# Attention and MoE kernel: the turned softmax weights laid out for 512-byte reads, with a second buffer, the last w_in columns kept in SBUF, and a new order of the steps

## The chip, the cores and the metric

The kernel runs on one core of a Trainium2 chip. The metric is the time of one execution on the device in microseconds (us), the median of several runs. One further execution was taken with the hardware profiler; all rows below are from it. The engines are TensorE (PE, with its weight loads PEld), VectorE (DVE), ScalarE (ACT), GpSimd (POOL) and SyncE (SP). Almost all DMAs are issued by SP, from one queue in order.

## The reference

```python
def _attn_ref(x, state):                    # x (8, 8, 512, 64), state (8, 8, 32, 64)
    scale = 1.0 / np.sqrt(D)
    scores = scale * np.matmul(x, state.transpose(0, 1, 3, 2))
    scores = scores - scores.max(-1, keepdims=True)
    a = np.exp(scores)
    a /= a.sum(-1, keepdims=True) + 1e-09
    xread = np.matmul(a, state)
    scores2 = scale * np.matmul(state, x.transpose(0, 1, 3, 2))
    ...
    a2 /= a2.sum(-1, keepdims=True) + 1e-09
    sread = np.matmul(a2, x)
    return np.concatenate([xread, sread], axis=2)

def _moe_ref(x, w_in, w_out):               # x (8 * 544, 512), w_in (512, 2048), w_out (2048, 512)
    h = np.maximum(x @ w_in, 0.0)
    return h * h @ w_out
```

The weights w_in and w_out come as 64-bit floats and are turned into 32-bit ones in the kernel ("decode").

## The kernel before, in words

There are nine blocks of rows: 512 rows of xread for each of the eight batches, and block 8 with the 8 x 32 rows of sread. To have matmuls at the fast rate and near full precision, an operand is split into a rounded part "hi" and the rest "lo", and three products are summed (mm3, L563; split, L539: the hi copy on ACT, the subtraction on POOL or DVE).

xread is never formed: state times w_in is made first ("w2", by batch and by block hb of 256 of the 2048 columns), and hidden (L1065) multiplies it with the softmax weights. w2 comes from three places. Batches 0 and 1: rows direct.hb, right from the decoded w_in tile wf (two_w2, L938). Batches 2 to 5: split_wf (L918) splits w_in, later_w2 (L982) multiplies, results w4ps, stored to DRAM through "o" tiles. Batches 6 and 7: rows w2.hb, from a second reload of w_in, stored as w2l. For the second and third use w_in is read back from DRAM (win_f, written by decode_wi) by load_wf 1 and 2 (L912) into one of two "wf" buffers.

The block hidden.b.fc makes 128 of the 2048 columns for one batch: six matmuls of 512 columns into a PSUM bank (ph, two banks), then on ACT and DVE relu, square, g_hi, and last g_lo, which releases the bank. accumulate.b.fc (L1121) follows with twelve matmuls into acc. Batches 4 to 7 use a form with fewer products (m34, m52, m76, m1).

The sread side: exp_s (L724) gives e, unnormalized. Its matmul with x (read, L811) wants e with positions on the partitions. transposes (L797) does this by way of DRAM: for each of two halves g, DVE transposes e in 32 x 32 blocks into a tile "turned", SP stores it to e_d, then four DMAs read it back as eT. The tile has one buffer:

```python
turned = p2.tile([P, S], F32, tag="turned", name=f"turned{b}_{g}", bufs=1)
nc.vector.transpose(turned, self.e2.pop(g))
nc.sync.dma_start(e_d[b][g], turned)
...
self.eT = p2.tile([P, KC, G * NC, Ns], F32, tag="eT", name=f"eT{b}", bufs=1)
```

Rows of PE (ROWS, L366) join groups of small matmuls that follow each other: scores.b, read.b, direct.hb and w2.hb, each group in one or two PSUM banks of ps_b ("psb") and ps_h ("ph").

The order is written out by hand. PLAN (L25) names the steps one by one; each name runs its step to the next yield, so the instructions of each engine and of SP's queue stand in that order. SECOND (L391) names the instructions that go to the other one of two engines: with decode_wi.p the clamp goes from DVE to POOL, with w_out_lo.fc the subtraction of prep_wo.fc (L1057) from POOL to DVE. Tiles are given out in rings: five "o" buffers for all stored results, two "wraw" buffers for raw w_in and wf_hi. A tile of a ring waits until the last use of its buffer is over; for a stored one that is the landing of its DMA. Nearly every call goes through L447, so profile rows are told apart by their tiles.

Of the kernel before, what the change touches and what calls it, by code (L numbers as in the profile page):

```python
# [25 lines left out]
    ident warm.0 warm.8 warm.19 warm.36 warm.21 start.0 warm.34 warm.29 warm.28 warm.14 load_states.0 load_states.0  # L26
        load_states.0 start.0 load.0.1 neg_ident load.0.1 warm.5 warm.13 prep.0.0 prep.0.0 states.0 states.0
        prep.0.1 prep.0.0 prep.0.1 prep.0.1 prep.0.0 prep.0.1 warm.24 load_raw.0 load_raw.1 start.1 start.1 warm.2
        warm.11 warm.22 load_wo.0 decode_wi.0 decode_wi.0 scores.0 load.1.1 load.1.1 load_raw.2 decode_wi.0
        decode_wi.0 warm.30 warm.32 decode_wi.0 keep_s.0.1 decode_wi.1 decode_wi.1 warm.35 keep_s.0.0 warm.25  # L30
        decode_wi.1 warm.1 decode_wi.1 prep.1.0 load_wo.1 prep.1.0 decode_wi.1 warm.15 transposed_scores.0.1
        transposed_scores.0.0 softmax.0.1 direct_w2.0 warm.33 softmax.0.0 warm.26 warm.23 direct_w2.0 direct_w2.0
        warm.31 softmax.0.1 warm.16 softmax.0.1 softmax.0.0 warm.6 direct_w2.0 direct_w2.0 load_wo.2 warm.37
        direct_w2.0 softmax.0.0 direct_w2.0 second_w2.0 prep_wo.0 softmax.0.1 warm.3 exp_s.0.0 warm.18 softmax.0.0
        prep_wo.0 prep_wo.0 warm.12 warm.20 second_w2.0 second_w2.0 warm.9 warm.4 decode_wi.2 prep.1.1 warm.27
        second_w2.0 second_w2.0 softmax.0.0 prep_wo.0 prep.1.1 load_raw.3 second_w2.0 softmax.0.1 warm.17 warm.7
        decode_wi.2 prep.1.1 prep.1.1 prep.1.0 softmax.0.1 decode_wi.2 decode_wi.2 softmax.0.0 prep.1.0 scores.1
# [24 lines left out]
        direct_w2.3 transposes.0 direct_w2.3 load_wo.12 decode_wi.10 direct_w2.3 direct_w2.3 load_raw.11
        decode_wi.10 decode_wi.10 decode_wi.10 hidden.1.3 hidden.1.3 hidden.1.3 hidden.1.3 hidden.1.3 prep_wo.6
        load_raw.9 decode_wi.8 prep_wo.11 prep_wo.11 prep_wo.11 decode_wi.8 decode_wi.8 second_w2.3 second_w2.3
        second_w2.3 decode_wi.8 states.2 prep_wo.11 hidden.0.7 hidden.0.7 hidden.0.7 prep_wo.11 prep_wo.5
        hidden.0.4 transposes.0 second_w2.3 hidden.0.7 split_states second_w2.3 second_w2.3 hidden.0.4 hidden.0.4
        hidden.0.4 accumulate.1.3 accumulate.1.3 accumulate.1.3 hidden.0.7 hidden.0.7 hidden.0.4 hidden.0.4
        hidden.0.5 accumulate.1.3 accumulate.1.3 accumulate.1.3 decode_wi.11 decode_wi.11 decode_wi.11 decode_wi.11
        decode_wi.8 decode_wi.9 hidden.0.5 hidden.0.5 exp_s.1.0 prep_wo.9 hidden.0.6 hidden.0.5 prep_wo.7
        accumulate.0.4 accumulate.0.4 prep_wo.9 prep_wo.8 decode_wi.9 decode_wi.9 decode_wi.9 decode_wi.11  # L70
        hidden.0.5 hidden.0.5 accumulate.0.5 hidden.0.6 hidden.0.6 hidden.0.6 load_raw.12 load_raw.14 exp_s.1.0
        hidden.0.6 hidden.0.6 decode_wi.9 direct.4+direct.5 prep_wo.8 prep_wo.8 prep_wo.8 load_wo.13 prep_wo.7
        prep_wo.7 prep_wo.8 direct_w2.5 direct_w2.5 direct_w2.5 decode_wi.12 direct_w2.5 exp_s.1.0 direct_w2.4
# [12 lines left out]
        direct_w2.6 decode_wi.14 accumulate.1.7 sread.0 sread.0 sread.0 load_wf.1.0 sread.0 prep_wo.10 hidden.0.9
# [278 lines left out]

ROWS = """  # L366
    scores.0
    scores.1
    direct.4 direct.5
    direct.6 read.0  # L370
    direct.7
    scores.2 read.1
    w2.1 scores.3
    read.2
    w2.0 scores.4
    read.3
    w2.2 scores.5
    w2.5 read.4
    w2.3 scores.6
    w2.6 read.5  # L380
    w2.4 scores.7
    w2.7 read.6
    read.7
"""

# [1223 lines left out]
```

## Time and profile before

| what | value |
|---|---|
| median of 3 runs | 647.99 us (647.28 to 649.07) |
| the profiled execution's own time | 647.67 us |
| its span | 645.9 us |
| PE busy | 631.8 us, 98% |
| DVE, ACT, POOL busy | 474.5, 419.7, 211.4 us |
| DMA | 149343 packets, 105.76 MB; 92960 packets under 512 B |
| HBM read, written | 69.27 MB, 35.65 MB |

The span is what the profiler saw of the engines; the execution's own time has some 1.8 us more around it. Busy time of PE is modelled: a row of a matmul runs into the next one, so that a wait of PE shows shorter than it is. A bracket behind a row of a timeline tells the idle time of the engine before it, and what ended it as far as the profile shows.

### The profile page before, as it was taken

How to read it: one execution, taken by the hardware profiler on the slowest of the kernel's cores; microseconds unless marked ns; L12 is line 12 of the kernel's file. 1: busy time of each engine (PE TensorE's matmuls, PEld its weight loads, DVE VectorE, ACT ScalarE, POOL GpSimd, SP SyncE). 2: the span in 40 equal slices, each digit the busy share in tenths (PEclk: the TensorE clock that was granted, in tenths of full speed). 3: DMA queues.
4: the chain of work that ended last, by engine and by line, in shares of the span. 5: the costliest groups of instructions: out<-in, count | busy, mean ns of one | idle time of the engine just before them, and what ended most of it. 6: DMA issues, size and time to landing. Idle time of an engine off the chain costs nothing.

```text
span 645.9 us, 12786 instructions
## 1 busy us (share of the span) xinstructions
PE 631.8 (98%) x4629; PEld 535.7 (83%) x4629; DVE 474.5 (73%) x968; ACT 419.7 (65%) x882; POOL 211.4 (33%) x206
## 2 busy tenths in 40 slices
PE   9999999999989999899999999999999999999996
PEld 7777767888767777677778888999999999999996
DVE  4999698655855686786677599998767776577556
ACT  4998775654653557455566679887766766667653
POOL 0365343432313142121221140004334275564430
PEclk9999999999999999899999999999999999999999
DMA  8977889988989888999897402120420040003001
GB/s 285 347 258 248 261 248 322 307 226 220 250 223 268 252 216 203 237 269 250 232 257 225 132 2 81 34 83 1 148 82 18 16 131 17 2 26 107 2 2 65
DMA packets 149343, 105.76 MB, mean 164 GB/s; under 512 B 92960, under 2 KB 122144, under 8 KB 149280
## 3 DMA queue, kind: packets, MB, share of 16 engines
q1 hardware_dynamic: 148992, 104.69, 56.5%
q8 instruction: 36, 0.59, 0.4%
q10 hardware_dynamic: 288, 0.26, 0.1%
q14 instruction: 27, 0.22, 0.1%
HBM read 69.27 MB, written 35.65 MB: 162 GB/s over the span
## 4 chain that ended last, share of the span: by engine, by line
PE 75%; DVE 7%; DMA 6%; issue 4%; ACT 3%; SPq 3%; POOL 1%; POOLq 0%; DVEq 0%; ACTq 0%
PE ph L447 25%; PE m L447 23%; PE acc L447 21%; SPq L447 3%; DMA e_d<-turned 2%; PE w2ps L447 2%; DVE wf L447 2%; DMA win_f<-wf 2%; PE w4ps L447 2%; DVE m L447 1%; DMA w_d<-w4o 1%; PE pr L447 1%; DMA wi_raw<-in_moe_w_in_dram 1%; DVE g_lo L447 1%; ACT ph L447 1%
## 5 line engine op out<-in xcount | busy, mean ns | idle before, releaser
L447 PE MATMUL ph<-k_hi,w 128*128 128x512 f32 x512 | 176.8, 394 | 1.3 <-DVE g_lo L447 1.3
L447 PE MATMUL acc<-wo,g_hi 128*128 128x512 f32 x576 | 165.2, 395 | 1.4 <-POOL wo L447 0.9
L447 PEld LDWEIGHTS acc<-wo,g_hi 128*128 128x128 f32 x576 | 107.1, 188 | 28.7 <-issue 3.8
L447 ACT ACTIVATE r<-ph 128x512 f32<-128x512 f32 (+1 forms) x124 | 70.1, 568 | 72.0 <-PE ph L447 68.0
L447 PEld LDWEIGHTS ph<-k_hi,w 128*128 128x128 f32 x512 | 96.5, 188 | 23.4 <-DVE g_lo L447 3.1
L447 PE MATMUL ph<-k_lo,w 128*128 128x512 f32 x256 | 100.5, 392 | 0.0
L447 PE MATMUL acc<-wo,g_lo 128*128 128x512 f32 x288 | 97.7, 393 | 1.9 <-DVE g_lo L447 1.9
L447 PEld LDWEIGHTS acc<-wo,g_lo 128*128 128x128 f32 x288 | 54.1, 189 | 14.3 <-DVE g_lo L447 2.3
L447 DVE TENSOR_TENSOR g_lo<-ph,g_hi 128x512 fp32r<-128x512 f32 (+1 forms) x79 | 49.5, 631 | 22.1 <-ACT g_hi L447 19.5
L447 PEld LDWEIGHTS ph<-k_lo,w 128*128 128x128 f32 x256 | 48.3, 189 | 7.5
L447 POOL TENSOR_TENSOR sp<-sp,m 128x512 f32<-128x512 f32 x22 | 23.3, 1061 | 94.8 <-DVE m L447 81.7
L447 POOL TENSOR_TENSOR w<-w_f,w 128x512 fp32r<-128x512 f32 x19 | 25.2, 1333 | 53.6 <-ACT w L447 35.6
L447 ACT CAST w<-w_f 128x512 fp32r<-128x512 f32 x56 | 34.3, 615 | 7.6 <-PE ph L447 6.0
L447 ACT ACTIVATE g_hi<-r 128x512 fp32r<-128x512 f32 (+1 forms) x60 | 33.9, 570 | 3.9 <-PE acc L447 2.7
L447 ACT ACTIVATE g<-r 128x512 f32<-128x512 f32 x54 | 33.8, 630 | 1.2 <-DVE s4.1.0_5062 L447 0.5
L447 POOL TENSOR_TENSOR wf<-wf,wf_hi 128x512 fp32r<-128x512 f32 x13 | 17.0, 1317 | 48.0 <-ACT wf_hi L447 48.0
L447 DVE TENSOR_TENSOR w<-w_f,w 128x512 fp32r<-128x512 f32 x37 | 27.8, 753 | 5.9 <-ACT w L447 5.8
L447 DVE SCALAR_TENSOR_TENSOR ph<-ph,r 128x512 f32<-128x512 f32 (+1 forms) x29 | 19.0, 656 | 14.6 <-ACT r L447 14.4
L447 ACT ACTIVATE ph<-ph 128x512 f32<-128x512 f32 x40 | 23.5, 587 | 5.6 <-issue 3.7
L447 POOL TENSOR_TENSOR wo<-dec,wo 128x512 fp32r<-128x512 f32 x13 | 17.5, 1347 | 22.1 <-ACT wo L447 22.1
L447 DVE COPY w4o<-w4ps 128x512 f32<-128x512 f32 x19 | 12.3, 686 | 12.6 <-PE w4ps L447 8.5
L447 DVE TENSOR_REDUCE m<-sp 128x16 f32<-128x512 f32 x28 | 18.6, 668 | 1.6 <-ACT sp L447 1.6
(1386 smaller groups left out, 1506.6 us busy)
## 6 DMA issues: line engine op xcount, KB each, us to landing
w_f<-w_d SPq DMA_DIRECT2D x40, 256.0 KB, 3.7
wi_raw<-in_moe_w_in_dram SPq DMA_DIRECT2D x16, 512.0 KB, 5.4
wo_raw<-in_moe_w_out_dram SPq DMA_DIRECT2D x16, 512.0 KB, 6.5
xr<-in_x_dram SPq DMA_DIRECT2D x16, 512.0 KB, 5.7
wf<-win_f SPq DMA_DIRECT2D x16, 512.0 KB, 5.0
w_d<-w4o SPq DMA_DIRECT2D x32, 256.0 KB, 4.5
out_dram<-o SPq DMA_DIRECT2D x30, 256.0 KB, 3.0
xp<-in_x_dram SPq DMA_DIRECT2D x96, 64.0 KB, 3.9
```

The costliest lines, as they stand in the source:

```text
L447: op = call(*args, **kw)
```

## The change

Turned e is written in an order in which the four pieces of 32 positions that one partition of eT wants lie side by side: a read fetches 512 bytes at a time where it was 128. The second half's tile is from batch 2 on in the space of sD, the states of batches 0 and 1, which are no longer needed then. Block 7 of w_in is not read back: row w2.7 follows direct.7 from the same decoded tile, then split_wf.7 splits it, with its lo part in a "wraw" buffer, and later_w2.7 runs before later_w2.0. PLAN and SECOND are new up to the middle of batch 4. PE has 4,001 instructions before and after, DVE 970 and 980, ACT 870 and 869, POOL 211 and 202, SP 450 and 448.

```diff
 ROWS:
-    direct.7
+    direct.7 w2.7
...
-    w2.7 read.6
+    read.6

 class Attention, transposes(self):
             for g in range(G):
-                turned = p2.tile([P, S], F32, tag="turned", name=f"turned{b}_{g}", bufs=1)
-                nc.vector.transpose(turned, self.e2.pop(g))
+                pool, tag = (cp, "sD") if g and b >= NX else (p2, "turned")
+                turned = pool.tile([P, S], F32, tag=tag, name=f"turned{b}_{g}", bufs=1)
+                nc.vector.transpose(turned.rearrange("p (j k n) -> p k j n", k=KC, n=Ns), self.e2.pop(g))
                 yield
                 nc.sync.dma_start(e_d[b][g], turned)
                 yield
-            self.eT = p2.tile([P, KC, G * NC, Ns], F32, tag="eT", name=f"eT{b}", bufs=1)
-            blocks = e_d[b].rearrange("g (c i) (k j n) -> j i k (g c) n", c=NC, k=KC, n=Ns)
+            self.eT = p2.tile([P, G * NC, KC, Ns], F32, tag="eT", name=f"eT{b}", bufs=1)
+            blocks = e_d[b].rearrange("g (c i) (j k n) -> j i (g c) k n", c=NC, k=KC, n=Ns)
             for j in range(4):
                 nc.sync.dma_start(self.eT[32 * j : 32 * j + 32], blocks[j])

 read():
-                                self.eT[:, k, NC * g + c], xn[:, h, k],
+                                self.eT[:, NC * g + c, k], xn[:, h, k],

 split_wf(hb):
-        lo = wf.pop(hb)
+        w = lo = wf.pop(hb)
         hi = p2.tile([P, NC, HB], F32R, tag="wraw", name=f"wf_hi{hb}", bufs=2)
+        if hb == NHB - 1:
+            lo = p2.tile([P, NC, HB], F32R, tag="wraw", name=f"wf_lo{hb}", bufs=2)
...
-            yield from split(hi[:, q], lo[:, q], lo[:, q].bitcast(F32), f"wf_lo.{hb}.{i}")
+            yield from split(hi[:, q], lo[:, q], w[:, q].bitcast(F32), f"wf_lo.{hb}.{i}")

 two_w2(hb, b0, pool, tag):
-        w = wf.pop(hb).bitcast(F32)
+        w = (wf[hb] if hb == NHB - 1 else wf.pop(hb)).bitcast(F32)

 needed(name):
-            "w2": [key("load_wf", 2, i), key("states", 2)],
+            "w2": [key("load_wf", 2, i) if i < NHB - 1 else key("decode_wi", 2 * i + 1), key("states", 2)],

 steps of block hb:
-        step(key("load_wf", 2, hb), load_wf, 2, hb, after=[key("split_wf", hb)])
-        step(key("load_wf", 1, hb), load_wf, 1, hb, after=needs if hb >= DH else [made])
-        step(key("split_wf", hb), split_wf, hb, after=[key("load_wf", 1, hb)])
+        whole = row[key("w2", hb)]
+        if hb < NHB - 1:
+            step(key("load_wf", 2, hb), load_wf, 2, hb, after=[key("split_wf", hb)])
+            whole = key("load_wf", 1, hb)
+            step(whole, load_wf, 1, hb, after=needs if hb >= DH else [made])
+        step(key("split_wf", hb), split_wf, hb, after=[whole])

 SECOND (two lines of it):
-    decode_wi: 4 7 8 11 12 15
+    decode_wi: 3 5 8 13 14
...
-    w_out_lo: 4 8 10
+    w_out_lo: 3 6 7 8 15
```

DVE, batch 4, the last row ahead of the second half's transpose (e24 is e of batch 4, aT and k_lo belong to the softmax weights, srall is sread). Before:

```order
L447 STREAM_TRANSPOSE aT4_0_3208<-sp4_0_3047 128x512
L447 STREAM_TRANSPOSE srall_74<-srd3_0_3204 128x2x32
L447 STREAM_TRANSPOSE srall_74<-srd3_1_3211 128x2x32
L447 TENSOR_TENSOR w2_3_1_3039<-w2_f3_1_3040,w2_3_1_3039 128x2x256
L447 STREAM_TRANSPOSE turned4_1_3258<-e24_3053 128x512
L447 TENSOR_TENSOR w2_3_2_3042<-w2_f3_2_3043,w2_3_2_3042 128x2x256
L447 TENSOR_TENSOR k_lo4_3207<-aT4_0_3208,k_hi4_3206 128x512
L447 TENSOR_TENSOR g_lo2_14_3242<-ph2_14_3157,g_hi2_14_3241 128x512
```

and now, from the first half's transpose on:

```order
L445 STREAM_TRANSPOSE turned4_0_3165<-e24_3014 128x4x4x32
L445 TENSOR_REDUCE m14_0_3046<-sp4_0_3007 128x16
L445 TENSOR_SCALAR m14_0_3046<-m14_0_3046 128x16
L445 RECIPROCAL m14_0_3046<-m14_0_3046 128x16
L445 STREAM_TRANSPOSE turned4_1_3205<-e24_3014 128x4x4x32
L445 STREAM_TRANSPOSE aT4_0_3218<-sp4_0_3007 128x512
L445 TENSOR_TENSOR g_lo2_13_3201<-ph2_13_3108,g_hi2_13_3200 128x512
L445 STREAM_TRANSPOSE xT5_1_3256<-xp5_1_2862 128x512 x2
L445 SCALAR_TENSOR_TENSOR ph2_15_3116<-ph2_15_3116,r2_15_3222 128x512
```

The first transpose stood ten rows above the piece of before (turned4_0, with a g_lo right behind it); now three small rows lie between the two, and the rows with g_lo follow both.

ACT, around the cast of wo7, the w_out rows that accumulate.0.7 needs (wf6 is block 6 of w_in being decoded, w2o are results of the direct rows). Before:

```order
L447 ACTIVATE dec7_1012<-dec7_1012 128x512
L447 CAST wo8_1101<-dec8_1031 128x512
L447 COPY w2o5_0_0_1103<-w2ps5_0_0_1060 128x512
L447 COPY w2o5_0_1_1106<-w2ps5_0_1_1061 128x512
L447 COPY w2o4_0_0_1113<-w2ps4_0_0_1058 128x512
L447 ACTIVATE wf6_1108<-wf6_1108 128x512
L447 COPY w2o4_0_1_1116<-w2ps4_0_1_1059 128x512
L447 CAST wo7_1138<-dec7_1012 128x512
L447 ACTIVATE ph1_5_1140<-ph1_5_1140 128x512 x2
L447 CAST g_hi1_5_1147<-ph1_5_1140 128x512
```

and now:

```order
L445 ACTIVATE dec8_1044<-dec8_1044 128x512
L445 CAST wo7_1105<-dec7_987 128x512
L445 COPY w2o4_0_0_1107<-w2ps4_0_0_1064 128x512
L445 COPY w2o4_0_1_1112<-w2ps4_0_1_1065 128x512
L445 CAST wo9_1115<-dec9_822 128x512
L445 COPY w2o5_0_0_1126<-w2ps5_0_0_1066 128x512
L445 COPY w2o5_0_1_1129<-w2ps5_0_1_1067 128x512
L445 ACTIVATE wf6_1134<-wf6_1134 128x512
L445 CAST wo8_1141<-dec8_1044 128x512
L445 ACTIVATE ph1_5_1144<-ph1_5_1144 128x512 x2
```

The cast has moved from behind wf6 and three w2o copies to before all of them.

PE, the first hidden blocks of batch 2 behind block 0 (ph2_3 is hidden.2.3). Before:

```order
L447 MATMUL ph2_3_2399<-k_lo2_1409,w2_2_1_1968 128x512
L447 MATMUL ph2_3_2399<-k_hi2_1408,w2_2_1_1968 128x512
L447 MATMUL ph2_2_2411<-k_hi2_1408,w2_2_1_1968 128x512
L447 MATMUL ph2_2_2411<-k_lo2_1409,w2_2_1_1968 128x512
L447 MATMUL ph2_2_2411<-k_hi2_1408,w2_2_1_1968 128x512 x2
L447 MATMUL ph2_2_2411<-k_lo2_1409,w2_2_1_1968 128x512
L447 MATMUL ph2_2_2411<-k_hi2_1408,w2_2_1_1968 128x512
L447 MATMUL ph2_5_2424<-k_hi2_1408,w2_2_2_2008 128x512
```

and now:

```order
L445 MATMUL ph2_2_2462<-k_lo2_1410,w2_2_1_2091 128x512
L445 MATMUL ph2_2_2462<-k_hi2_1409,w2_2_1_2091 128x512
L445 MATMUL acc2_0_0_2446<-wo1_510,g_hi2_1_2388 128x512 x2
L445 MATMUL acc2_0_0_2446<-wo1_510,g_lo2_1_2389 128x512
L445 MATMUL acc2_0_1_2447<-wo1_510,g_hi2_1_2388 128x512 x2
L445 MATMUL acc2_0_1_2447<-wo1_510,g_lo2_1_2389 128x512
L445 MATMUL acc2_0_2_2448<-wo1_510,g_hi2_1_2388 128x512 x2
L445 MATMUL acc2_0_2_2448<-wo1_510,g_lo2_1_2389 128x512
L445 MATMUL acc2_0_3_2449<-wo1_510,g_hi2_1_2388 128x512 x2
L445 MATMUL acc2_0_3_2449<-wo1_510,g_lo2_1_2389 128x512
L445 MATMUL ph2_5_2483<-k_hi2_1409,w2_2_2_2096 128x512
```

Where hidden.2.3, 2.2 and 2.5 followed each other, accumulate.2.1 now stands between hidden.2.2 and 2.5, and 2.3 comes behind 2.5.

## Rows read from the trace of the kernel before

**Rows 1.** The page: span, busy time of each engine, DMA tenths in 40 slices.

```profile
span 645.9 us, 12786 instructions
...
PE 631.8 (98%) x4629; PEld 535.7 (83%) x4629; DVE 474.5 (73%) x968; ACT 419.7 (65%) x882; POOL 211.4 (33%) x206
...
DMA  8977889988989888999897402120420040003001
```

**Rows 2.** Windows: length; busy PE, PEld, DVE, ACT, POOL; granted clock, DMA share, GB/s.

```profile
160.00:340.00 180.00, 174.93 (x1534) 134.79 (x1535) 123.72 (x251) 98.01 (x194) 45.37 (x39) 0.99 0.92 241
...
400.00:500.00 100.00, 100.00 (x701) 93.77 (x700) 82.58 (x191) 73.59 (x163) 26.27 (x31) 1.00 0.21 62
```

**Rows 3.** Timeline of PE: start, length, what, idle time before it and its releaser.

```profile
67.15 0.51 PE L447 MATMUL ph<-k_hi,w 128*128 128x512 f32 x1 [0.45 <-DVE g_lo L447]
...
82.37 0.49 PE L447 MATMUL acc<-wo,g_hi 128*128 128x512 f32 x1 [0.53 <-ACT wo L447]
83.72 0.50 PE L447 MATMUL acc<-wo,g_hi 128*128 128x512 f32 x1 [0.85 <-POOL wo L447]
...
183.48 0.38 PE L447 MATMUL w4ps<-wf_hi,s 64*128 64x256 f32 x1 [1.20 <-DVE g_lo L447]
...
191.02 0.50 PE L447 MATMUL ph<-k_hi,w 128*128 128x512 f32 x1 [0.86 <-DVE g_lo L447]
...
196.68 0.38 PE L447 MATMUL w4ps<-wf_hi,s 64*128 64x256 f32 x1 [0.27 <-DVE g_lo L447]
...
197.88 0.38 PE L447 MATMUL w4ps<-wf_hi,s 64*128 64x256 f32 x1 [0.16 <-DVE w4o L447]
...
250.47 1.10 PE L447 MATMUL pr<-xr,eT 128*32 128x64 f32 x64 [0.74 <-ACT g_hi L447]
...
258.21 0.39 PE L447 MATMUL acc<-wo,g_lo 128*128 128x512 f32 x1
258.44 0.61 PE L447 MATMUL acc<-wo,g_hi 128*128 128x512 f32 x2
260.91 0.50 PE L447 MATMUL acc<-wo,g_lo 128*128 128x512 f32 x1 [1.85 <-DVE g_lo L447]
```

**Rows 4.** Windows, the stretch after the longest wait; columns as in rows 2.

```profile
261.80:265.40 3.60, 3.60 (x32) 2.16 (x38) 0.94 (x2) 0.33 (x1) 0.00 (x0) 0.55 0.98 239
```

**Rows 5.** Timeline of DVE: the second transpose of batch 4, and g_lo.

```profile
258.37 0.71 DVE L447 STREAM_TRANSPOSE turned<-e 128x512 f32<-128x512 f32 x1 [4.96 <-DMA e_d<-turned]
...
260.17 0.69 DVE L447 TENSOR_TENSOR g_lo<-ph,g_hi 128x512 fp32r<-128x512 f32 x1
```

**Rows 6.** Timeline of SP's queue in the same stretch: issue of DMAs.

```profile
243.19 4.39 SPq L447 DMA_DIRECT2D eT<-e_d  x4
...
251.93 0.38 SPq L447 DMA_DIRECT2D e_d<-turned  x1
```

**Rows 7.** Tiles eT, w4o, xp, turned: ns min/median/max, first and last start.

```profile
L447 SPq DMA_DIRECT2D eT<-e_d x32: 562/674/3288, 63.1 to 332.8; - x32
DMA to landing us min/median/max: 3.1/4.2/6.4
...
L447 SPq DMA_DIRECT2D w_d<-w4o x32: 359/440/1465, 124.7 to 217.7; - x32
DMA to landing us min/median/max: 3.2/4.5/7.0
...
L447 SPq DMA_DIRECT2D xp<-in_x_dram x96: 578/635/1831, 101.6 to 299.2; - x96
...
  DMA e_d<-turned: 10.9, 5
```

**Rows 8.** Timelines of ACT and POOL ahead of the wait for wo7.

```profile
80.69 0.63 ACT L447 ACTIVATE wf<-wf 128x512 f32<-128x512 f32 x1 [3.45 <-POOL wf L447]
...
78.72 1.94 POOL L447 TENSOR_SCALAR wf<-wi_raw 128x512 f32<-128x512 f32 x1 [9.89 <-DMA win_f<-wf]
```

**Rows 9.** The chain that ended last: the first of later_w2's groups on PE.

```profile
121.76 1.62 PE w4ps L447 x24
```

More of the change, by code (lines that the diff above doesn't have):

```diff
@@ L391 @@
 SECOND = """
-    b_lo: 4.6.0 4.7.0 4.7.1 5.0.0 5.1.1 5.3.0 5.3.1 5.5.1 5.6.1 5.7.1 6.0.0 6.1.1 6.3.0 6.3.1 6.5.1 6.7.0 7.3.1
-        7.4.1
-    d_sum: 4.6.0 4.6.1 5.1.0 5.3.0 5.3.1 5.4.0 6.1.1 6.5.0 6.5.1 6.6.1 7.0.0 7.1.1 7.4.0 7.5.0 7.6.0 7.6.1
-    decode_wi: 4 7 8 11 12 15
-    decode_wo: 4 6 8 9 13 14
+    b_lo: 4.6.1 5.0.0 5.1.1 5.3.0 5.3.1 5.5.1 5.6.1 5.7.1 6.0.0 6.1.1 6.3.0 6.3.1 6.5.1 6.7.0 7.3.1 7.4.1
+    d_sum: 4.7.1 5.1.0 5.3.0 5.3.1 5.4.0 6.1.1 6.5.0 6.5.1 6.6.1 7.0.0 7.1.1 7.4.0 7.5.0 7.6.0 7.6.1
+    decode_wi: 3 5 8 13 14
+    decode_wo: 5 6 8 11 13
     eT: 2.1 4.1 6.0 7.1
-    e_sum: 4.6.1 5.4.1 5.7.0 6.0.0 6.0.1 6.1.0 6.1.1 6.4.1 6.5.0 6.5.1 6.7.1 7.1.0 7.1.1 7.2.1 7.3.0 7.3.1 7.4.0
-    f_lo: 4.6.1 4.7.0 5.0.1 5.1.0 5.2.1 5.4.0 5.4.1 5.5.1 6.0.0 6.1.0 6.2.0 6.2.1 6.3.0 6.6.0 6.7.0 6.7.1 7.0.0
+    e_sum: 4.7.0 5.4.1 5.7.0 6.0.0 6.0.1 6.1.0 6.1.1 6.4.1 6.5.0 6.5.1 6.7.1 7.1.0 7.1.1 7.2.1 7.3.0 7.3.1 7.4.0
+    f_lo: 4.5.1 4.6.1 5.0.1 5.1.0 5.2.1 5.4.0 5.4.1 5.5.1 6.0.0 6.1.0 6.2.0 6.2.1 6.3.0 6.6.0 6.7.0 6.7.1 7.0.0
         7.1.1 7.2.1 7.3.1 7.5.0
-    f_sum: 4.7.1 5.0.0 5.2.1 5.3.0 5.7.0 6.0.1 6.1.0 6.2.0 6.3.0 6.4.0 6.4.1 6.5.1 6.6.1 6.7.1 7.0.0 7.0.1 7.2.0
-        7.4.0 7.4.1 7.5.0 7.6.0
-    first: 1.1
+    f_sum: 5.0.0 5.2.1 5.3.0 5.7.0 6.0.1 6.1.0 6.2.0 6.3.0 6.4.0 6.4.1 6.5.1 6.6.1 6.7.1 7.0.0 7.0.1 7.2.0 7.4.0
+        7.4.1 7.5.0 7.6.0
+    first: 1.0
     g_pe: 0.1
@@ L407 @@
         7.8 7.9 7.10 7.11 7.12 7.14
-    k_lo: 0.1 1.0 1.1 2.0 2.1 3.0 4.0 4.1 5.0 5.1 6.0 6.1 7.0 7.1
-    keep_s: 0.0
-    last_out: 1.0 2.0 3.1 6.0 7.1
-    out: 2.3 3.0 3.3 4.0 5.1 5.3 6.2 7.0 7.1 7.2
-    p_lo: 5.0.0 5.0.1 5.3.1 5.4.0 5.7.1 6.0.1 6.1.0 6.3.1 6.4.1 6.7.1 7.0.0 7.0.1 7.4.1 7.6.0
+    k_lo: 0.1 1.0 1.1 4.1 5.0 5.1 6.0 6.1 7.0 7.1
+    keep_s: 0.1
+    last_out: 2.1 3.0 3.1 4.0 6.1 7.1
+    out: 2.2 2.3 4.0 5.1 5.3 6.2 7.0 7.1 7.2
+    p_lo: 4.4.0 4.6.0 5.0.0 5.0.1 5.3.1 5.4.0 5.7.1 6.0.1 6.1.0 6.3.1 6.4.1 6.7.1 7.0.0 7.0.1 7.4.1 7.6.0
     part: 0.1 0.3 1.0 1.3
```

697 lines of the change are left out of this document (348 added, 349 removed), and 4 rows, old and new, of the table SECOND.

## The prediction

> **What bounds the kernel now.** I read the page first: TensorE (PE) is busy for 631.8 of 645.9 us, while the DMA line stands at 8 and 9 for the first half and near 0 after it [rows 1]. The second view is the table of windows. In 400:500 PE is busy all the time, and the 16 DMA engines only 0.21; in 160:340 PE loses five microseconds and DMA stands at 0.92 [rows 2]. So the second half is PE at its rate, and no removed transfer can shorten it. What can be gained lies before 340 us, in the places where PE stands still.
>
> The third view is PE's timeline, where each row with a bracket is such a place [rows 3]. The reader is to see nine waits of 0.16 to 1.85 us and whom each waits for. How much one costs: two neighbours start 0.23 us apart (258.21, 258.44), a matmul's row is 0.39 long, so 0.16 of each idle time hides under the modelled end of the matmul before. I add 0.16 to each bracket: 0.61 (at 67.15), 0.69 and 1.01 (82.37, 83.72), 1.36 (183.48), 1.02 (191.02), 0.43 and 0.32 (196.68, 197.88), 0.90 (250.47) and 2.01 (260.91). Together 8.4 us. Then the clock: in the 3.6 us after the longest wait the granted clock is 0.55, part of them at the lower of its two levels, 1.2 instead of 2.4 GHz, with PE busy throughout; that costs 3.6 x 0.45 = 1.6 us [rows 4]. So 10.0 us are to be had, 1.5% of the time.
>
> **The change, part by part.** PE carries the same 4,001 instructions in both kernels; 24 of them read the same numbers from another tile. Its own work costs the same, and every term is a wait.
>
> 1. The second half of turned e gets its own buffer. Before, DVE stands at the second transpose of batch 4 for 4.96 us until the first half's store has landed, and the g_lo that PE wants comes three instructions later, at 260.17 [rows 5]. The store is late in turn: SP issues it only at 251.93, behind a 4.39 us group of eT reads and more [rows 6]. With a buffer of its own the second transpose has nothing to wait for; both halves then need stores of the batch before, long landed. Of five such waits, 10.9 us of DVE, only this one reaches PE [rows 7]. Gone: 2.0 us, and with the wait the fall of the clock, 1.6. For batches 0 and 1 the tile sD still holds states, so their second transposes keep the old wait; they did not stop PE.
>
> 2. Reads of eT in pieces of 512 bytes. By the code one read moves 1,024 pieces of 128 bytes before and 256 of 512 after. Its issue on SP took 0.67 us in the median, 3.3 at most; the w4o stores, which have 256 pieces, took 0.44 [rows 7]. These two are my ends, and I take 0.44, the row with the same count: 32 x 0.23 = 7.5 us of SP's queue, more where it stood full, since the group of four then takes 1.8 and not 4.39 us [rows 6]. For PE this matters at 250.47: the group of four eT reads of batch 3 is issued by 247.6 [rows 6], and a read lands 3.1 us after its issue at the earliest [rows 7], so it is this read, not the ACT cast that the bracket names, which ends the wait. Issued 2.6 us sooner it is in time; but the new order also puts this row of PE 18 matmuls (4.1 us) earlier. Against that stands that SP now issues both stores of e one behind the other, where eight other DMAs stood between. Gone: 0.9 us, with less certainty.
>
> 3. The last w_in columns are kept: two reads of 512 KB less on SP. No bracket of PE names them; nothing either way. In exchange the two matmul groups of block 7 stand in one row, and its split and later_w2 come first of the eight and no longer last: to before 121.76 us, where the first of them ran [rows 9]. ACT, DVE, POOL and the five "o" buffers are in use there already, and on SP six stores (two w2l, four w4o) move there too. That is the price to watch, below.
>
> 4. The new order. At 82 us PE waited for wo7, first its cast on ACT, then its subtraction on POOL [rows 3]. ACT was late because wf6 stood before it, and wf6 waited 3.45 us for POOL, which had waited 9.89 us for a store of w_in to free its buffer [rows 8]. Now the cast of wo7 stands six places ahead of wf6, and the subtraction is on DVE. Gone: 1.7 us. The wait for the buffer moves to DVE (the clamp of decode_wi.12); behind it stand g_lo of hidden 1.5 and 1.4, which PE needs 16 matmuls (3.6 us) later: covered. At 67 and 191 us a hidden block waits for the PSUM bank of the block two before it, that is for that block's g_lo. Now eight accumulating matmuls more (1.8 us) stand between at the first place and twelve (2.7 us) at the second: gone, 0.6 and 1.0 us.
>
> 5. What stays. Hidden 2.0 still stands directly before later_w2.4, whose second half takes its bank: 1.36 us stay. The pair later_w2.5 and 6 is unchanged: 0.75 stay.
>
> 6. What comes. Ten more instructions on DVE, nine fewer on POOL, one fewer on ACT. The transposes write four runs per row instead of one. No row shows that form; the ends are 0.71 us as now [rows 5] and twice that, and I take 0.71, for no element is added. At 1.42 the twelve transposes after 160 us would add 8.5 us to a DVE that is busy 124 of 180 us [rows 2], so mostly in its gaps. New waits of PE I can only bound: nothing, or as much as all that go. I take 1.4 us, one and a half of the middle wait above (0.90).
>
> **Sum.** 0.6 + 1.7 + 1.0 + 0.9 + 2.0 + 1.6 = 7.8 us less, 1.4 more: 6.4 less. The profiled execution took 647.67 us, its span 645.9; that makes 641.3, and the median of the runs shown is 0.3 above that execution: **641.6 us**.
>
> **Rivals.**
> - *The issue of an eT read does not get shorter.* For it: an xp load has half as many pieces as an eT read and takes 0.64 us [rows 7], so count alone does not set it. Against it: the w4o stores at 0.44 [rows 7]. The Trainium skill (DMA: Bandwidth & Descriptors, Anatomy of one DMA) states of DMAs issued by GpSimd that many descriptors can be emitted before their incremental cost shows up; by that rule the issue would stay as it is. The trace agrees between 512 and 1,024 pieces, and not below [rows 7]. Then the 0.9 of part 2 stays: 642.5. Chance 0.15.
> - *Only the buffer helps.* The new order has its own list of waits, as long as the old one, in other places. For it: the nine waits have five different causes, and a new order meets them anew; DMA stands at 0.92 [rows 2], so landings vary from 3.1 to 6.4 us for one and the same read [rows 7]. Against it: the three places of part 4 are mended by distances that are counted in matmuls. Then only 3.6 go: 644.4. Chance 0.17.
> - *No change.* A wait of over 2 us comes again at another store, with the clock falling behind it: 3.6 back, and the rest as in the rival before: 648.0, within 0.3%. Chance 0.11.
> - *Slower, by the "o" buffers.* In the 16 us before 121.76 [rows 9] twelve tiles (four partial sums, two w2o, two w2l, four w4o) go through five buffers, each held until its store lands. With w4o's median landing of 4.5 us they just pass. If the stores land as the latest do, at 7.0 [rows 7], each of three rounds is 2.5 us later, and these tiles hold PSUM banks that PE needs: 7.5, and 1.6 for the clock, on top of the forecast: 650.7. It decides where PE's cover, 12 matmuls before later_w2.7 and 8 behind it (4.5 us), is used up: from landings of about 6 us. Chance 0.07.
> - The forecast itself: 0.50.
>
> **How the numbers follow.** A measurement of this kernel tells about 0.3% (1.9 us) from no change. Forecast, the first rival and "only the buffer" are faster by more: 0.82; no change 0.11; slower 0.07. The range: at its low end all 10.0 us go and none come, 638.0; at its high end only the buffer helps and one wait of 2.1 us is new, 646.5. That leaves out the lower two cases, 0.18.
>
> **What would show it.** In the profile of the changed kernel: no wait of DVE for e_d from batch 2 on; eT's issue near 0.44 us; no bracket for wo7 or for the third of three hidden blocks; later_w2.4 still waiting 1.2 us; a granted clock of 1.00 between 20 and 640 us. I am wrong if the waits of PE before 340 us add up to more than 5 us, if a fall of the clock remains, or if time comes after 400 us.

## The result, and the profile after

In the first comparison the changed kernel takes **642.09 us** (median of 4 runs, 640.26 to 642.74) against 647.63 (647.02 to 649.07): a ratio of 0.9907, interval 0.988 to 0.9933. On a second chip, beside 21 runs of the kernel before, the ratio is 0.9909 (0.9878 to 0.9939; 640.12 against 646.61 us). The forecast was 641.6 us, 638.0 to 646.5. The profiled execution took 642.74 us, its span is 641.0.

The page of the changed kernel: span, busy time of each engine, granted clock and DMA in tenths of 40 slices.

```profile
span 641.0 us, 12771 instructions
...
PE 629.1 (98%) x4629; PEld 535.4 (84%) x4629; DVE 479.7 (75%) x978; ACT 421.6 (66%) x881; POOL 201.6 (31%) x197
...
PEclk9999999999999999999999999999999999999999
DMA  8998888999979799999864401220420040003001
...
DMA packets 124479, 104.71 MB, mean 163 GB/s; under 512 B 60160, under 2 KB 97536, under 8 KB 124416
```

Of the 92960 packets under 512 bytes 32800 are gone: 32 reads of 1,024 pieces, and 32 more.

The windows of [rows 2] and one around the old long wait: length; busy PE, PEld, DVE, ACT, POOL; granted clock, DMA share, GB/s.

```profile
160.00:340.00 180.00, 176.36 (x1510) 137.49 (x1507) 129.10 (x258) 99.98 (x197) 47.32 (x39) 1.00 0.88 233
240.00:270.00 30.00, 28.21 (x223) 21.86 (x221) 20.41 (x42) 17.29 (x35) 6.89 (x6) 1.00 0.93 235
400.00:500.00 100.00, 100.00 (x699) 93.63 (x698) 81.45 (x188) 73.15 (x162) 26.49 (x30) 1.00 0.21 64
```

As forecast, nothing comes or goes in 400:500. In 160:340 PE loses 3.6 us where it lost 5.1 [rows 2], and the clock stands at 1.00 throughout.

The timeline of PE: start, length, what, idle time before it and its releaser. From 16 to 640 us these five, from 185.26 on, are all the rows with a bracket; the two before them are of the start.

```profile
12.92 0.66 PE L445 MATMUL px<-ident,xn 128*128 128x128 f32 x4 [0.77 <-DMA xn<-in_x_dram]
...
15.38 1.10 PE L445 MATMUL w2ps<-wf,sD 64*32 64x256 f32 x32 [0.27 <-DVE wf L445]
...
185.26 0.38 PE L445 MATMUL w4ps<-wf_hi,s 64*128 64x256 f32 x1 [1.20 <-DVE g_lo L445]
...
200.50 0.35 PE L445 MATMUL w4ps<-wf_hi,s 64*128 64x256 f32 x1 [0.16 <-DVE w4o L445]
201.01 0.38 PE L445 MATMUL w4ps<-wf_hi,s 64*128 64x256 f32 x1 [0.15 <-DVE w4o L445]
...
231.86 0.50 PE L445 MATMUL ph<-k_hi,w 128*128 128x512 f32 x1 [0.34 <-ACT w2l L445]
...
269.99 0.73 PE L445 MATMUL acc<-wo,g_hi 128*128 128x512 f32 x2 [1.78 <-DVE o L445]
```

Set against [rows 3]: the brackets at 67, 82, 84, 191, 250 and 261 are gone. The one of later_w2.4 stays at 1.20, that of later_w2.5 and 6 has shrunk. New are 231.86 and 269.99, and the start: the same w2ps row began at 14.05 before and begins at 15.38 now, behind a load of x that lands late. The row in the kernel before, first as it stands in its profile, then in the second one that is told of below:

```profile
14.05 1.10 PE L447 MATMUL w2ps<-wf,sD 64*32 64x256 f32 x32
...
14.94 1.10 PE L447 MATMUL w2ps<-wf,sD 64*32 64x256 f32 x32 [0.15 <-DVE wf L447]
```

So 0.9 of these 1.3 us come and go without any change to the kernel.

The new long wait, read from DVE, then from SP's queue:

```profile
260.40 0.69 DVE L445 COPY w2l<-w2ps 128x512 f32<-128x512 f32 x1 [1.64 <-PE w2ps L445]
...
269.24 1.30 DVE L445 COPY o<-acc 128x512 f32<-128x512 f32 x2 [3.09 <-DMA w2a_d<-w2l]
```

```profile
254.64 4.71 SPq L445 DMA_DIRECT2D xp<-in_x_dram  x4
259.39 2.92 SPq L445 DMA_DIRECT2D eT<-e_d  x4
262.36 0.45 SPq L445 DMA_DIRECT2D wf<-win_f  x1
262.91 3.00 SPq L445 DMA_DIRECT2D w2a_d<-w2l  x2
```

Two of batch 2's partial sums want "o" buffers; w2l, the results for batches 6 and 7, holds them until it is stored. Its copies (one on DVE, one on ACT) were done by 261.1, the stores are issued from 262.91 on and land 6.2 to 6.4 us later. That is the pattern of the old wait [rows 5, 6] with another tile.

The tiles eT and turned after (ns min/median/max, first and last start):

```profile
L445 SPq DMA_DIRECT2D eT<-e_d x32: 318/450/1637, 57.5 to 324.8; - x32
DMA to landing us min/median/max: 2.7/4.4/6.3
...
L445 DVE STREAM_TRANSPOSE turned<-e x16: 654/693/705, 44.9 to 318.1; 128x512 f32<-128x512 f32 x16
```

An eT read is issued in 0.450 us in the median (0.674 before [rows 7]), a transpose with four runs per row takes 0.693 us, and no wait of DVE for e_d is left.

### The profile page after: what moved, and what is told of

Same layout as the page of the kernel before. It is cut to its first block, busy times and chain, and to the rows that moved or that the text cites. A ratio compares the mean times of both kernels' runs of the same rounds, so it can differ in the third digit from the quotient of the medians.

```text
span 641.0 us, 12771 instructions
## 1 busy us (share of the span) xinstructions
PE 629.1 (98%) x4629; PEld 535.4 (84%) x4629; DVE 479.7 (75%) x978; ACT 421.6 (66%) x881; POOL 201.6 (31%) x197
## 4 chain that ended last, share of the span: by engine, by line
PE 81%; DVE 6%; DMA 4%; issue 3%; SPq 2%; ACT 2%; POOL 0%; POOLq 0%; DVEq 0%; ACTq 0%
PE ph L445 28%; PE acc L445 24%; PE m L445 23%; SPq L445 2%; PE w4ps L445 2%; PE w2ps L445 2%; DMA w_f<-w_d 2%; DVE wf L445 1%; PE pr L445 1%; DVE g_lo L445 1%; DMA wi_raw<-in_moe_w_in_dram 1%; DMA w2a_d<-w2l 1%; DVE m L445 1%; ACT ph L445 1%; PE pw L445 1%
## 5 line engine op out<-in xcount | busy, mean ns | idle before, releaser
L445 POOL TENSOR_TENSOR w<-w_f,w 128x512 fp32r<-128x512 f32 x20 | 26.7, 1341 | 73.6 <-ACT w L445 66.5
L445 POOL TENSOR_TENSOR sp<-sp,m 128x512 f32<-128x512 f32 x20 | 21.5, 1073 | 80.1 <-DVE m L445 75.0
L445 DVE SCALAR_TENSOR_TENSOR ph<-ph,r 128x512 f32<-128x512 f32 (+1 forms) x34 | 21.5, 633 | 18.2 <-ACT r L445 18.0
L445 POOL TENSOR_TENSOR wo<-dec,wo 128x512 fp32r<-128x512 f32 x11 | 14.5, 1325 | 37.0 <-ACT wo L445 37.0
L445 ACT COPY w4o<-w4ps 128x512 f32<-128x512 f32 x16 | 9.1, 585 | 15.2 <-PE w4ps L445 11.8
L445 DVE STREAM_TRANSPOSE xT<-xp 128x512 f32<-128x512 f32 x24 | 15.8, 689 | 4.3 <-PE st L445 2.5
```

What stands on the lines that cost most here:

```text
L445: op = call(*args, **kw)
```

## The experiments

All ratios are to the kernel before, run beside each variant on the same chip.

**The parts, in the old order and in the new one.** The first run takes the kernel before and adds the second buffer:

```diff
+                pool, tag = (cp, "sD") if g and b >= NX else (p2, "turned")
-                turned = p2.tile([P, S], F32, tag="turned", name=f"turned{b}_{g}", bufs=1)
+                turned = pool.tile([P, S], F32, tag=tag, name=f"turned{b}_{g}", bufs=1)
```

> The kernel before, its old order and its 128-byte reads kept; only the second half of turned e gets the sD space from batch 2 on. Theory of the prediction: the 4.96 us wait of DVE at the second transpose of batch 4 goes, with it PE's 2.0 us wait at 260.9 and the fall of the granted clock behind it (1.6 us): 3.6 us less, a ratio to the kernel before of 0.9944. Rival A: the fall of the clock has another cause than the wait and stays: 2.0 us less, 0.997. Rival B: the wait only moves to the next thing that is late: no change, 1.000. In the profile: no wait of DVE for e_d from batch 2 on, and a granted clock of 1.00 in 261 to 266 us.

Measured: 644.5 against 645.75 us, ratio 0.998 (0.9959 to 1.0001). The theory's 0.9944 lies outside; both rivals' ratios lie within. Between the profiled executions the difference is larger, 644.50 us against 647.67 and 647.54, since the two of the kernel before lie above its median of 645.75. In the profile both waits of [rows 3] at 250 and 261 are gone, and the clock is 1.00 in 261.8:265.4. The wait at 250 was to go by the other part of the change. DVE's and SP's rows of batch 3, before:

```profile
236.54 0.71 DVE L447 STREAM_TRANSPOSE turned<-e 128x512 f32<-128x512 f32 x1 [2.12 <-DMA e_d<-turned]
...
234.49 0.82 SPq L447 DMA_DIRECT2D w2a_d<-w2l  x1
...
237.89 1.26 SPq L447 DMA_DIRECT2D xp<-in_x_dram  x2
239.24 0.57 SPq L447 DMA_DIRECT2D e_d<-turned  x1
...
243.19 4.39 SPq L447 DMA_DIRECT2D eT<-e_d  x4
```

and with the second buffer, DVE, SP, and a new wait of PE:

```profile
234.43 0.67 DVE L447 STREAM_TRANSPOSE turned<-e 128x512 f32<-128x512 f32 x1
...
232.48 0.61 SPq L447 DMA_DIRECT2D w2a_d<-w2l  x1
...
237.28 0.57 SPq L447 DMA_DIRECT2D e_d<-turned  x1
...
241.10 4.59 SPq L447 DMA_DIRECT2D eT<-e_d  x4
...
278.34 1.10 PE L447 MATMUL w2ps<-wf,sT 64*32 64x256 f32 x32 [1.28 <-DMA wf<-win_f]
```

Store and reads come 2.0 and 2.1 us sooner, and read.3 does not wait, though its group of reads takes as long as before (4.59 and 4.39 us). That DVE's wait of 2.12 us had made them late is not shown, and SP's rows speak against it: the transpose was done at 237.25, while SP was busy with other loads until 239.15, and SP was 2.0 us later already at the w2l store, 234.49 against 232.48, ahead of that transpose. The two profiles without the buffer have this wait (0.74 and 0.73 us), the two with it in the old order do not; why SP was ahead in these is open. In return a reload of wf is late at 278.

The second run adds the layout:

```diff
-                nc.vector.transpose(turned, self.e2.pop(g))
+                nc.vector.transpose(turned.rearrange("p (j k n) -> p k j n", k=KC, n=Ns), self.e2.pop(g))
...
-            blocks = e_d[b].rearrange("g (c i) (k j n) -> j i k (g c) n", c=NC, k=KC, n=Ns)
+            blocks = e_d[b].rearrange("g (c i) (j k n) -> j i (g c) k n", c=NC, k=KC, n=Ns)
...
```

> As the run before, and eT is read in pieces of 512 bytes; the old order is kept, and the last w_in columns are still reloaded. Theory: the issue of an eT read falls from 0.67 to about 0.45 us, the group of four ahead of read.3 takes 1.8 to 2 us and not 4.4, and PE's wait of 0.90 us at 250.5 goes: 0.9 us less than with the buffer alone, a ratio to the kernel before of 0.993. Rival: this wait is set by something else (the ACT cast which the bracket names), and stays: the ratio of the run before, 0.9944. The transpose that writes four runs per row should stay near 0.70 us.

Measured: 642.66 us, 0.9948 (0.993 to 0.9966), 1.8 us less than the run before. The theory's 0.993 and the rival's 0.9944 both lie within the interval, but the rival meant by its number that nothing is added to the buffer, and the buffer alone had measured 0.998. The wait for wf at 278 is gone, where SP's group of eT reads ahead of it took 1.90 us and not 4.54:

```profile
261.27 1.90 SPq L447 DMA_DIRECT2D eT<-e_d  x4
```

So the layout is worth something, by shortening SP's queue as far as these two profiles show, but not at read.3, which did not wait in the run before either.

The changed kernel with one buffer, with the old layout, and with both (the two diffs above, backwards):

> The changed kernel, but both halves of turned e in one buffer again. Theory: in the new order the second transpose follows the first closely, and SP issues the first store up to 5 us behind its transpose; so DVE stands 3 to 9 us in each of the batches 2 to 7, together 25 to 37 us, and PE loses at least the 3.6 us that the buffer was to save, up to 15: a ratio to the kernel before of 0.997 to 1.014 (0.991 for the changed kernel). Rival: the gain is the order's, which has room enough for the old wait: 0.991 to 0.993.

> The changed kernel, but turned e in its old layout, so that eT is read in pieces of 128 bytes. Theory: the issue of a read goes back to about 0.67 us and a group of four to 2.7 to 4.4 us; in the changed kernel the last read of batch 3 is issued 6.1 us before read.3 begins, so 2.6 us later it lands 0.5 to 1.5 us too late there, and nowhere else: 0.5 to 1.5 us more than the changed kernel, a ratio to the kernel before of 0.992 to 0.993. Rival: the new order alone has removed that wait, and nothing changes: 0.991.

> The changed kernel with one buffer and the 128-byte layout again: only the new order and the kept block of w_in are left of the change. Theory: the order is written for the second buffer, so that it is a loss without it, as in the run with one buffer; with longer issues in SP's queue on top, it is that run's 664 us or up to 4 us more. Rival: the two do not add, since DVE waits for the store anyway: 660 to 664 us.

Measured: one buffer 664.01 us, 1.0276 (1.0246 to 1.0305); the old layout 644.52 us, 0.997 (0.9947 to 0.9992); both 668.59 us, 1.0356 (1.0301 to 1.0412). With one buffer the 28.0 us of DVE are as the theory had them, but PE loses more than the 15 us that were its upper end. With the old layout as well the ratio is 0.8% higher again, slightly more than the theory had there. The tile turned, PE's waits from 20 to 345 us (what for; us in total, times, longest) and the windows of 240:270 and 270:345:

```profile
  DMA e_d<-turned: 28.0, 6
...
PE ph L445 <- DVE g_lo L445: 11.9, 5, 4.8
PE w4ps L445 <- DVE g_lo L445: 3.9, 2, 2.9
...
240.00:270.00 30.00, 24.92 (x161) 19.62 (x160) 22.88 (x45) 16.68 (x32) 12.62 (x10) 0.94 0.90 233
270.00:345.00 75.00, 67.53 (x628) 49.78 (x627) 46.80 (x101) 35.91 (x72) 12.70 (x11) 0.95 0.74 206
```

The granted clock is 0.94 and 0.95 there, which is 0.06 of 30 and 0.05 of 75 us, some 5.5 us more. With the old layout and two buffers the ratio lies above the theory's 0.993 and the rival's 0.991, both outside the interval; and in the profile the price is not at read.3, which has no bracket, but at the new wait near 270. PE, the window behind it, and SP:

```profile
272.44 1.22 PE L445 MATMUL acc<-wo,g_hi 128*128 128x512 f32 x2 [3.97 <-DVE o L445]
...
270.80:277.60 6.80, 5.16 (x54) 2.90 (x58) 5.19 (x13) 0.24 (x1) 2.10 (x2) 0.52 1.00 272
...
261.40 4.64 SPq L445 DMA_DIRECT2D eT<-e_d  x4
266.09 0.66 SPq L445 DMA_DIRECT2D wf<-win_f  x1
266.85 0.89 SPq L445 DMA_DIRECT2D w2a_d<-w2l  x2
```

The group of reads begins 2.0 us later and takes 4.64 us for 2.92, the w2l stores go out 3.9 us later than with the layout, PE waits 4.0 us and the clock falls. This profile is of the slowest of twelve executions (647.67 us), so how much of the median's loss lies here is not shown. **The parts do not add.** The buffer is worth 0.2% in the old order and 3.7% in the new one (1.0276 against 0.9908, the mean of the changed kernel's two ratios); the new order without buffer and layout is a loss of 3.6%. With both parts the new order and the kept block give 0.9908 where the old order gives 0.9948, 2.6 us; the intervals of the two just overlap, and no run tells the order from the kept block.

**The same two kernels again**, with no edit.

> The changed kernel once more, unaltered, on the chip and beside the runs of before on which its variants run, and with a second profile. Theory: its gain is made of waits that the profile names, so the second profile shows them again: 1.2 us at later_w2.4, and the wait for the partial sums' copies near 270 us, whose length (1.8 us in the first profile) hangs on when two w2l stores land; a ratio to the kernel before of 0.990 to 0.995. Rival: the first comparison flattered it, since the kernel before had the fall of the clock in all of its few runs there: 0.995 to 0.998.

> The kernel before once more, unaltered, with a second profile. Theory: PE's wait for the second transpose of batch 4 (1.85 us in the first profile) and the fall of the clock behind it are there again, and its time is some 3 us above the variant with a buffer of its own. Rival: the wait differs from execution to execution, since it hangs on the landing of one store, and the clock falls only where it is long: a wait under 1.5 us and a granted clock of 1.00 behind it.

Measured: the changed kernel 640.12 us, 0.9909 as given above, so that the rival's 0.995 to 0.998 is refuted; the kernel before 647.54 us in its one execution. In the second profile of the changed kernel the wait at 270 is not there (the two w2l stores land 2.2 and 4.3 us after their issue, and DVE copies from 266.94 on), that of later_w2.4 is, and one at 55.9 us is new. The kernel before, second profile: PE twice, then DVE, then the window of [rows 4].

```profile
251.02 1.10 PE L447 MATMUL pr<-xr,eT 128*32 128x64 f32 x64 [0.73 <-ACT g_hi L447]
261.00 0.50 PE L447 MATMUL acc<-wo,g_lo 128*128 128x512 f32 x1 [1.38 <-DVE g_lo L447]
...
258.46 0.71 DVE L447 STREAM_TRANSPOSE turned<-e 128x512 f32<-128x512 f32 x1 [4.50 <-DMA e_d<-turned]
...
261.80:265.40 3.60, 3.60 (x57) 1.96 (x55) 1.71 (x3) 1.01 (x2) 0.00 (x0) 1.00 1.04 248
```

DVE's wait is 4.50 and not 4.96, PE's 1.38 and not 1.85, and the clock does not fall. The fall is no fixed part of the wait, and a wait that ends with a landing had another length in each execution. The time is the same all the same, 647.54 and 647.67 us: this execution lost 0.9 us at the start and has a wait of 0.39 us for wf at 280.8 that the other has not. The kernel before spreads over 642.1 to 650.3 us in these comparisons.

**Two transfers put back.** The changed kernel, with two copies of block 7 of w_in:

```diff
+    def again(i):
+        nc.sync.dma_start(spare[i], win_f[NHB - 1][:, : NC * HB])
...
 PLAN:
-    later_w2.5 load.4.1
+    again.0 later_w2.5 load.4.1
...
-    accumulate.3.7
+    accumulate.3.7 again.1
```

> The changed kernel with two transfers more on SP: 512 KB each, from block 7 of w_in in DRAM to an unused place in DRAM, where the kernel before issued its two reloads of that block (in later_w2.4's stretch near 190 us, and behind accumulate.3.7 near 300 us). They read what the reloads read and also write it, so they cost the DMA engines at least as much. Theory of the prediction: the reloads that were left out were worth nothing, so nothing changes: a ratio to the kernel before of 0.991. Rival: the DMA engines stand at 0.85 to 0.93 there and have no room; at 240 GB/s each copy holds them 2.2 us for the read and as much for the write, what is queued behind comes later, and PE loses 2 to 6 us: 0.994 to 1.000.

Measured: 641.44 us, 0.9932 (0.9904 to 0.996). The profile shows no wait that the changed kernel doesn't have in one of its two profiles, but for 0.24 us at read.2; the interval holds both the theory and the lower end of the rival. With the changed kernel at 0.9908 the copies cost at most 3.4 us (0.996 against it); whether it is nothing isn't told.

**Mending what the profile names.** First, the w2l stores of block 2 ahead of the reads:

```diff
 PLAN:
-    load.6.1 load.6.1 transposes.4 sread.3
+    load.6.1 load.6.1 sread.3
...
-    load_wf.2.5 w2.2+scores.5
+    w2.2+scores.5
...
-    accumulate.2.15 last_w2.2
+    accumulate.2.15 last_w2.2 transposes.4 load_wf.2.5
```

> The changed kernel, but the two w2l stores of block 2 stand on SP ahead of the four eT reads of batch 4 and of the reload of block 5 of w_in, no longer behind them. Theory: these stores hold the buffers that the partial sums of batch 2 want; issued at 261 to 262 us in place of 262.9 to 266, they land by 267, DVE's 3.1 us wait ends 2 us sooner, and PE's 1.8 us (1.9 with the part under the end of a matmul) at 270 goes: 1.0 to 1.9 us less than the changed kernel. Rival: SP is full there, and the wait goes over to the reload of block 5 or to eT, which are now 2 us later: no change, with a bracket that names wf or eT.

Measured: 642.13 us, 0.9936 (0.9913 to 0.9958), 2.0 us above the changed kernel beside it and not 1.0 to 1.9 below. The wait at 270 is gone, and two others are there; PE's rows, and the DVE wait behind the first:

```profile
286.84 0.50 PE L445 MATMUL ph<-k_hi,w 128*128 128x512 f32 x1 [1.86 <-DVE g_lo L445]
...
296.46 1.10 PE L445 MATMUL pr<-xr,eT 128*32 128x64 f32 x64 [1.48 <-DMA wf<-win_f]
...
283.86 0.71 DVE L445 STREAM_TRANSPOSE aT<-sp 128x512 f32<-128x512 f32 x1 [3.27 <-DMA a_d<-aT]
```

The second row reads eT and no wf, which its bracket names: the four eT reads of its batch, issued from 287.33 on, land 7.1 to 7.4 us later, the last of them as the row begins. aT is the next tile with one buffer whose store stands in SP's queue. So the next run gives it a second one:

```diff
-                aT = p2.tile([P, S], F32, tag="aT", name=f"aT{b}_{g}", bufs=1)
+                tag, n = ("wraw", 2) if g else ("aT", 1)
+                aT = p2.tile([P, S], F32, tag=tag, name=f"aT{b}_{g}", bufs=n)
```

> The run with the two w2l stores first on SP, and besides a buffer of its own for the second half of aT in batches 5 to 7 (in the space of the raw w_in, free by then), as the change gave one to the second half of turned e. In that run DVE stood 6.1 us in three places until aT's first half was stored, once 3.3 us, with PE's wait of 1.9 us near 286 us behind it. Theory: a tile with one buffer whose store goes through SP's full queue is the pattern behind these waits; the 6.1 us fall to under 1, the wait at 286 goes, and the time falls by 1.5 to 2 us against that run: a ratio to the kernel before of 0.990 to 0.991, level with the changed kernel. Rival: the landing of the stores is only the last of several things late there (the load of wf ahead of read.5 is another, 1.5 us), and the wait goes over to them: 0.993 as in that run.

Measured: 642.71 us, 0.9939 (0.9915 to 0.9963). The waits for a_d and the one at 287 are gone as the theory has it, and the time is the rival's. Of the 1.86 us saved there the wait ahead of read.5 has taken 0.94, and one of 0.57 us for wf at 269.71 is new:

```profile
296.71 1.10 PE L445 MATMUL pr<-xr,eT 128*32 128x64 f32 x64 [2.42 <-DMA wf<-win_f]
```

Three places at once: the stores as in the first of these runs, and later_w2.4 and the start by these edits (parts of the lines of PLAN):

```diff
 PLAN:
-    start.1 load_wo.0 warm.8 warm.7 start.1 load.1.1
+    start.1 warm.8 warm.7 start.1 load.1.1 load_wo.0
...
-    accumulate.1.14 accumulate.1.15
+    accumulate.1.14 later_w2.4 later_w2.4 later_w2.4 later_w2.4 accumulate.1.15
...
-    accumulate.1.15 later_w2.4 hidden.2.1
+    accumulate.1.15 hidden.2.1
...
-    later_w2.4 later_w2.4 later_w2.4 hidden.2.2 load_wf.1.6
+    hidden.2.2 load_wf.1.6
```

> As the run before, and two more places of the changed kernel mended: the matmuls of later_w2.4 stand before hidden.2.1 and no longer directly behind hidden.2.0, and at the start the third load of w_out is issued behind the x loads of batch 1 and not before two of them. Theory: each wait that the profile of the changed kernel names is worth its length: 1.9 (partial sums), 1.4 (later_w2.4) and 1.3 (the start, where w2ps began at 15.4 and not 14.1 us) go, 4.6 us less than the changed kernel, 637 to 639 us where that takes 642. Rival: as the nine waits of before did, those mended come again elsewhere: at most 2 us less.

Measured: 644.07 us, 0.9968 (0.9945 to 0.9991): about 4 us more than the changed kernel, not 4.6 less. The wait of 1.20 is gone from its place, and at the start the w2ps row begins at 15.00 us, not at 14.1 as meant. PE's waits to 345 us are now, among others:

```profile
PE acc L445 <- ACT g_hi L445: 1.4, 1, 1.4
...
PE w4ps L445 <- ACT e L445: 0.8, 1, 0.8
```

The first is made by the move itself: accumulate.2.0 now follows directly on hidden.2.0, whose g_hi it wants, where later_w2.4 had stood between them. The second is later_w2.4's own at its new place. So the 1.20 us did not go, they changed their owner.

Last, another queue:

```diff
-            nc.sync.dma_start(w2a_d[hb][:, :, ts(g, HB)].rearrange("b p f -> p b f"), o)
+            nc.scalar.dma_start(w2a_d[hb][:, :, ts(g, HB)].rearrange("b p f -> p b f"), o)
```

> The changed kernel, but the 16 w2l stores are issued by ACT and not by SP, so that they stand behind no reads. Theory: the waits that come and go between 220 and 300 us come from SP's one queue in order, in which a store that frees a buffer stands behind reads that wait for room; with the stores elsewhere the o buffers come free 2 to 4 us sooner: 0.5 to 2 us less than the changed kernel, a ratio to the kernel before of 0.988 to 0.990. Rival: the DMA engines themselves are full, so the stores land no sooner, and the issue now holds ACT, on which g_hi stands: 0 to 3 us more, 0.991 to 0.996.

Measured: 644.99 us, 0.9998 (0.9975 to 1.0022), the rival, by a way of its own. The stores land in 3.7 us in the median, little sooner than the 4.0 to 4.1 on SP, and their issue takes ACT 0.37 us; but a store of a tile that DVE copies stands in ACT's order, and the casts of w come behind it:

```profile
281.48 0.39 ACTq L445 DMA_DIRECT2D w2a_d<-w2l  x1
281.91 1.14 ACT L445 CAST w<-w_f 128x512 fp32r<-128x512 f32 x2 [6.28 <-DMA xp<-in_x_dram]
...
289.22 0.50 PE L445 MATMUL ph<-k_hi,w 128*128 128x512 f32 x1 [1.94 <-DVE g_lo L445]
```

The casts of w stood at 275.5 in the second profile of the changed kernel. DVE's copies were at 278.25 and 279.56; why ACT went on only at 281.48 the profile doesn't settle. Six us late is also the sp behind them, and through it DVE's g_lo, for which PE waits at 289.

That the stores gain so little by another queue agrees with the Trainium skill (DMA: Bandwidth & Descriptors, Queues, rings and completion order), by which the queues of SP and ACT feed the same 16 DMA engines: in 240:290 these stood at 0.90 here too.

No version here has a lower ratio than the changed kernel.

## Why the prediction came out

The total, its sign and its range were right, and the likeliest case is the one that came. That the median lies within 0.5 us of the forecast is luck: step by step terms were off both ways, and in part they cancelled. The signs that were to show it came. The sign of being wrong that was nearest is the sum of PE's waits before 340 us, with its bound of 5 us: from 20 us on they add up to 4.4 us in the first profile (brackets and 0.16 each), and to 5.7 with the start, which the forecast did not count.

1. *The buffer, 2.0 and 1.6 for the clock.* The mechanism is right: in both profiles of the changed kernel, and in those of the two runs with the buffer in the old order, this wait and the fall are gone. The size is not. Alone, in the old order, the buffer saved 1.3 us in the median (at most 2.6 by the interval) for the 3.6 forecast. The 1.6 us were no fixed price: the second profile of before has the wait without the fall. And the price was taken from an execution of 647.67 us, where the median beside this run is 645.75. Whether the difference lies in the executions of before that had a shorter wait isn't shown, for only two of them have a profile. That "only this one reaches PE" is not refuted: read.3's wait went with the buffer too, but by SP's rows not through DVE's wait in batch 3.

2. *The layout, 0.9 at read.3.* The issue is 0.450 us for a forecast 0.44, a group of four 1.8 to 3.1 us. The Trainium skill's rule of the first rival, on which the issue would not shorten (DMA: Bandwidth & Descriptors, Anatomy of one DMA, stated there of GpSimd), does not hold for SP between 256 and 1,024 pieces by this row (0.450 against 0.674 us). The failing step is the place: "so it is this read" was right of the end of the wait and wrong of what made the read late, which was not the length of the group. The first read went out at 243.19, when the store of 239.24 had landed 3.9 us after its issue, and a group as long that began 2.1 us sooner did no harm. What the layout gives, 1.8 us in the old order and about 4 in the new one (0.997 against 0.9908), went in the profiles to what stands behind the reads in SP's queue: the reload of wf, the w2l stores.

3. *Two reads of w_in less: nothing.* Not refuted; the copies put back cost between nothing and 3.4 us.

4. *The order, 0.6 + 1.7 + 1.0.* The three places carry no bracket in either profile of the changed kernel. That the order is worth 3.3 us less what it brings, 1.4, fits the 2.6 us between the two orders with both parts; clear of noise this is not.

5. *What stays.* later_w2.4 waits 1.20 us, as stated; of the pair's 0.75 us 0.63 are left.

6. *What comes, 1.4.* This term was too small. The transposes cost nothing more, as taken, but the new waits come to 1.9 at 270 and 0.5 at 232 (brackets and 0.16 each) and 1.3 at the start: 3.7 us in the first profile, and with the start and waits at 56 us 3.0 in the second. Of the 1.3 at the start 0.9 may be no work of the change, as the kernel before had them in its second profile. By this count the profiled execution would be at 643.5 and not at 641.3; it took 642.74, and where the other 0.8 us went is not shown. The forecast added 0.3 for a median above the profiled execution, as the three runs of before had it; here the median lies 0.65 below. So an error of 1.4 us in the profiled execution became one of 0.5 in the median.

*The rivals.* That only the buffer helps is refuted by 0.998 against 0.9948 and 0.9908. "No change", a long wait at another store, came true for a part: the wait at 270 is such a one, 1.8 us in one of two profiles, without a fall of the clock; with the old layout it is 4.0 us with it. The "o" buffers did run short, not in the 16 us ahead of later_w2's first group but at batch 2's partial sums, and with a landing of 6.2 to 6.4 us, as the rival's condition had it.

## What to carry to other kernels

Here the DMA engines stood at 0.9 and one queue issued nearly everything; a tile with one buffer, a store in that queue and a landing of 2 to 8 us made a wait that moved on when it was mended. In such a place price a second buffer, a shorter issue and an order together, for the buffer was worth 0.2% in the old order and 3.7% in the new one, the layout 0.3 and 0.6%. Follow a late store to all who stand behind it, the reads of what it stores above all, and look what the queue did ahead of the store before an engine's wait is named as the cause. And read two profiles of one kernel before a landing's length goes into a sum.

## What was not expected of the hardware

The same wait of PE, 1.38 and 1.85 us in two executions of one program, had the granted clock at 1.00 behind it once and at 0.55 the other time; behind one of 1.78 us in the changed kernel it stayed at 1.00 as well, around the end of one of 3.97 us it was 0.52 for 6.8 us. Two w2l stores at the same place of the changed kernel landed 6.2 and 6.4 us after their issue in one profile, 2.2 and 4.3 in the other. And the 90 executions of the kernel before spread over 8 us, the ten of the changed one over 4.
